# Chunks of 128, 256, 44 times 512 and 384 tokens in a fused RG-LRU and FFN kernel, with the first twenty chunks ordered anew

## The chip, the cores and the metric

The kernel runs on one core of one Trainium2 chip. The metric is the device time of one execution in microseconds (us); the smaller, the better. A core has five engines that run their own instruction streams in order and meet at semaphores: PE (TensorE, the matrix multiplier), DVE (VectorE), ACT (ScalarE), POOL (GpSimd) and SP (SyncE, which here only issues DMAs).

## The reference

Two stages. First a gated linear recurrence over the tokens of each of 4 sequences of 5,824 tokens and 256 channels, then a feed-forward network (FFN) over all 23,296 tokens without an activation function:

```python
sig_r = 1.0 / (1.0 + np.exp(-r_gate))
sig_i = 1.0 / (1.0 + np.exp(-i_gate))
log_a = c * sig_r * np.log(np.clip(a_base, 1e-06, 1.0 - 1e-06))[None, None, :]
a_t = np.exp(log_a)
norm = np.sqrt(np.maximum(1.0 - a_t * a_t, 1e-06))
x_gated = norm * sig_i * x
for t in range(S):
    h = a_t[:, t] * h + x_gated[:, t]
    y[:, t] = h
...
a = x @ w1
b = x @ w2
h = a * b @ w3
return (h @ w_out).astype(np.float32)
```

In the second part `x` is the `y` of the first. w1 and w2 are 256 x 1024, w3 is 1024 x 1024, w_out is 1024 x 256. Since nothing stands between w3 and w_out, the kernel multiplies them once ("the fold", wp = w3 @ w_out) and uses the product. Inputs and output are float32, the matrix products run in bfloat16.

## The kernel before

The tokens are cut into chunks (`sizes`, L50). For each chunk a chain of jobs runs, and each job has a letter:

- `r`, `i`, `x` (L133) load the three inputs with one DMA each. `R` and `I` take the tanh on ACT (the sigmoid is made of it), `p` adds 1 on POOL, `t` multiplies by x in two halves on POOL (for the chunks in `DV_TIMES` in one step on DVE; halves in `DV_HALF` on DVE).
- `V` and `U` turn the results from tokens on partitions to channels on partitions. The chunks in `TURN_R` and `TURN_U` are turned on PE, by transposes of 128 x 128 into PSUM (L180); the others by one DMA transpose (L192).
- `d` (exp, ACT) makes the decay a, for each of two blocks of 128 channels; `s` squares it (POOL, or DVE or ACT by the sets `DV_SQUARE` and `AC_SQUARE`); `q` takes the root (ACT, with another function table, so a table load stands before it and another after it); `g` multiplies (DVE); `h` is the scan on DVE, which starts from the last column of the chunk before; `y` casts to bfloat16 on POOL (`DV_CAST`, `AC_CAST`: on DVE or ACT).
- `a` and `b` multiply by w1 and w2 on PE. The 1,024 hidden columns are four pairs of 128-column blocks; `ac.m.q` fills one PSUM slot with one block, `bc.m` fills two. `c` copies a's block out of PSUM (ACT, or DVE for `DV_COPY`), and `m` multiplies it by b's on DVE. `D` multiplies 128 tokens by wp, 8 matmuls of 256 columns; `e` copies two such results out (ACT, or DVE for `DV_EVAC`), `o` stores them.
- `L`, `C` load and cast the weights; `Ft`, `Fc`, `Fm`, `Fe` do the fold for one of 8 row blocks of w3: transpose, copy, multiply, scale into wp. `W` is a run of 8 matmuls without use, put where PE would wait.

Two things rule what runs when. `ORDER` (L438) is one written list of all jobs: each engine executes its own jobs in exactly this order, so a job that waits holds up all that follows on its engine. And `RINGS` (L102) says how many buffers a kind of tile has: the turned r and u, the a blocks, the D results and the fold's results share four PSUM slots ("po"), the b results and W share two ("pb"), the loads have four or five. A job that takes a buffer waits until the job that last read it is done. The weights pass through the buffers of a and nrm.

SP issues every DMA, in order. Its queue holds the loads, the DMA transposes and the stores.

The first chunks hold 256 tokens each, the last 256. wp must be complete before the first `D`, so the early part of the kernel is the FFN's first half for chunks 0 to 2, the fold and the gates of the next chunks.

Of the kernel before, what the change touches and what calls it, by code (L numbers as in the profile page):

```python
# [22 lines left out]
def kernel(  # L23
# [26 lines left out]
    sizes = [256, 256] + [CT] * 44 + [256]  # L50
# [29 lines left out]
    TURN_R = {0, 1, 2, 3, 4, 7, 12}  # L80
    TURN_U = {0, 1, 2, 3, 4, 5, 6, 7}
    DV_TIMES = {0, 1}
    DV_PLUS = set()
    DV_HALF = {(2, 0)}
    DV_SQUARE = {(0, 0), (1, 0), (10, 0)}
    AC_SQUARE = {(1, 1), (2, 0), (2, 1), (3, 0), (4, 0), (4, 1), (6, 0), (8, 1), (9, 1), (11, 0), (11, 1), (12, 1),
        (13, 0), (13, 1), (14, 0), (14, 1), (15, 1)}
    DV_CAST = set()
    AC_CAST = {4}
    DV_COPY = {(0, 0, 0), (0, 1, 0), (0, 1, 1), (0, 3, 0), (1, 1, 0), (1, 1, 1), (1, 2, 0), (1, 2, 1), (1, 3, 0), (2,  # L90
        0, 1), (2, 1, 0), (2, 1, 1), (2, 3, 0), (3, 0, 1), (3, 2, 0), (3, 2, 1), (4, 0, 0), (4, 1, 0), (4, 2, 0), (4, 2,
        1), (5, 1, 1), (5, 2, 1), (6, 2, 0), (6, 2, 1), (6, 3, 1), (7, 0, 0), (7, 1, 1), (7, 3, 0), (7, 3, 1), (8, 1, 0),
        (8, 2, 0), (9, 1, 0), (9, 1, 1), (9, 2, 1), (10, 0, 0), (10, 1, 0), (10, 1, 1)}
    DV_EVAC = {(1, 0), (2, 0), (3, 1), (5, 1), (9, 0), (9, 1)}
    FOLD_ACT = {('c', 7), ('e', 0), ('e', 1), ('e', 2), ('e', 3), ('e', 7)}
    W_ACT = {('w2', 0), ('w3', 6)}
    W_DVE = {('w1', 1)}
    STAGE = {'w1': ['a', 'a'], 'w2': ['nrm', 'nrm'], 'wo': ['a', 'nrm'], 'w3': ['a', 'nrm', 'a', 'nrm', 'a', 'nrm',
        'a', 'nrm']}
    CASTING = set()  # L100
    WARM = [8, 8, 8, 8, 8, 8, 8, 8, 8, 8, 8, 8, 8, 8, 8, 8]
# [59 lines left out]
    def times(c, half):  # L161
        n = sizes[c] // P
        fused = c in DV_TIMES
        if half == 0 or fused:
            T["u", c] = ring(gates, [P, NCB, 4, P], BF16, name="u_t", tag="u")
# [34 lines left out]
    def decay(c, cb):  # L200
        w = sizes[c]
        if cb == 0:
            T["a", c] = ring(held, [P, NCB, CT], F32, name="a_t", tag="a")
        a, pr = T["a", c][:, cb, :w], T["pr", c][:, cb, :w]
        if long_rows(c):
            a, pr = in_time(a), turned(pr)
        nc.scalar.activation(out=a, in_=pr, func=AF.Exp, scale=la4[:, cb:cb + 1], bias=la4[:, cb:cb + 1])  # L207

    def square(c, cb):
        w = sizes[c]  # L210
        if cb == 0:
            T["n", c] = ring(held, [P, NCB, CT], F32, name="nrm", tag="nrm")
# [23 lines left out]
    def scan(c, cb):  # L236
        w = sizes[c]
        if cb == 0:
            T["h", c] = ring(ypool, [P, NCB, CT], F32, name="h_t", tag="h")
        h, a, n = (T[key, c][:, :, :w] for key in "han")  # L240
        if cb == 0:
            for b in range(1, B):
                if 0 < b * S - starts[c] < w:
                    nc.vector.memset(a[:, :, b * S - starts[c]:b * S - starts[c] + 1], 0.0)
# [47 lines left out]
    def product(c, mp):  # L292
        w = sizes[c]
        if mp == 0:
            T["g", c] = ring(ffn, [P, KD, CT], BF16, name="g_t", tag="g")
        nc.vector.tensor_mul(out=T["g", c][:, 2 * mp:2 * mp + 2, :w], in0=T["sa", c, mp][:, :, :w],  # L296
                             in1=T["pb", c, mp][:, :, :w])

    def down(c, j):
        if c == NCH - 1:  # L300
            T["po_last", j] = po = ring(psum_o, [P, D], F32, name="po", tag="po")
        else:
            if j % 2 == 0:
# [7 lines left out]
    def evac(c, j2):  # L311
        T["ot", c, j2] = ring(ffn, [P, 2, D], F32, name="ot", tag="ot")
        copy_to((c, j2) in DV_EVAC, T["ot", c, j2], T["po", c, j2])

    def evac_last(c, j):
        if j % 2 == 0:
# [7 lines left out]
    def store(c, j2):  # L324
        t0 = starts[c] + 2 * j2 * P
        nc.sync.dma_start(out=out[t0:t0 + 2 * P, :].rearrange("(j p) c -> p j c", p=P),
                          in_=T["ot", c, j2])
# [36 lines left out]
    def fold_t(mi):  # L364
        pt = ring(psum_o, [P, KD, P], BF16, name="ptw", tag="po")
# [51 lines left out]
    def last(c):  # L417
# [21 lines left out]
        r0 r1 E A3. A0. A1. i1 R1 R0 W3 V1 I1 V0 W13 W12 A2. W9 d1.0 d1.1 s1.0 i0 W15 I0 x0 t0.1 W14 d0.0 s0.0 s1.1  # L439
        d0.1 s0.1 q0 x1 t1.1 Lw1.0 r3 Lw2.0 r2 q1 R3 Lw1.1 i2 W11 U0 g0 h0.0 Lw2.1 Cw1.0 W10 W2 U1 W0 W7 R2 W4 h0.1  # L440
        Lw3.2 x2 g1 y0 W8 Lwo.0 Cw2.0 a0.1.0 a0.1.1 h1.0 c0.1.0 h1.1 a0.0.0 a0.0.1 V2 c0.1.1 d2.0 c0.0.0 W6 y1 b0.0
        c0.0.1 d2.1 I2 Cw1.1 a1.0.1 a1.0.0 b0.1 a1.1.0 a0.2.0 c1.0.0 c1.0.1 Cw2.1 p2 a0.2.1 Cw3.2 m0.0 m0.1 c1.1.0
        Lwo.1 b1.0 m1.0 t2.0 r4 W1 c0.2.0 a1.1.1 a0.3.0 t2.1 Cwo.0 W5 c1.1.1 Ft2 c0.2.1 a1.3.0 s2.0 b1.1 c0.3.0 b0.2
        U2 a1.3.1 s2.1 Cwo.1 i3 Fc2 V3 x3 Lw3.0 q2 Lw3.1 i4 Lw3.4 m1.1 c1.3.0 Fm2 R4 g2 h2.0 h2.1 d3.0 Lw3.7 c1.3.1
        m0.2 d3.1 Lw3.5 Fe2 a1.2.0 a0.3.1 b1.2 a1.2.1 I3 c0.3.1 V4 s3.0 d4.0 d4.1 b0.3 y2 c1.2.0 Cw3.0 c1.2.1 m1.2
        a2.0.0 a2.1.0 b1.3 m0.3 a2.2.0 b2.0 m1.3 a2.2.1 c2.0.0 Lw3.3 a2.0.1 s4.0 c2.2.0 s3.1 p3 t3.0 c2.1.0 Cw3.1 Ft0
        c2.0.1 c2.2.1 Fc0 m2.0 Cw3.4 b2.1 I4 s4.1 q4 r7 t3.1 a2.3.0 a2.1.1 Fm0 b2.2 p4 Cw3.5 c2.1.1 Ft4 c2.3.0 m2.1
        Fe0 Ft1 a2.3.1 U3 Lw3.6 q3 Fc4 c2.3.1 Fc1 Fm4 Cw3.7 b2.3 Ft5 g3 Fe4 Fc5 Ft7 x4 Cw3.3 R7 r5 h3.0 h3.1 Fm1 Fm5
        Fc7 Fe5 Ft3 Fm7 Fe1 Cw3.6 V7 Fe7 y3 Ft6 Fc3 d7.0 d7.1 Fc6 m2.2 Fm3 i6 r6 a3.1.0 Fe3 R5 Fm6 a3.1.1 c3.1.0
        c3.1.1 t4.0 Fe6 t4.1 i7 i5 x5 U4 a3.0.0 R6 D0.0 a3.0.1 D0.1 I6 c3.0.0 e0.0 m2.3 g4 a3.3.0 a3.2.0 b3.0 h4.0  # L450
# [24 lines left out]
        D9.0 b11.3 D9.1 a12.0.1 m11.2 D9.2 m11.3 D9.3 b12.0 y13 x17 R18 d17.0 c12.0.0 c12.0.1 e9.0 m12.0 I17 a12.2.0
# [133 lines left out]
```

## Time and profile before

| | us |
|---|---|
| median of 3 runs | 516.77 |
| lowest and highest run | 515.22, 517.76 |
| span of the profiled execution | 513.8 |
| PE, ACT, DVE, POOL busy in it | 499.8, 465.5, 430.6, 312.9 |
| first FFN matmul starts | 12.97 |
| last store lands | 513.8 |

The profile shows one execution, instruction by instruction. Its span runs from the first to the last instruction; for this execution no other time is given, and the median of the runs is 3.0 us above the span. A row of the timeline is: start, length, engine, line, operation, output and inputs, shapes, how many were merged, and in brackets the idle time of the engine before it with what ended it. `L268` is line 268. Busy time is the time in which an instruction of the engine is under way, though two may overlap. In the first 60 us, the DMA view shows 280 to 425 GB/s from 3 us to about 44 us.

### The profile page before, as it was taken

Reading aid. Unit: us, or ns where it says so; the run is one execution under the profiler, and the core shown is the slowest. Engines: PE = TensorE matmul, PEld = TensorE weight load, DVE = VectorE, ACT = ScalarE, POOL = GpSimd, SP = SyncE. Lnnn points to the kernel's source line nnn. Section 1 sums busy time; section 2 is a strip of 40 time slices with the busy share of each in tenths; the row PEclk is TensorE's granted clock in tenths of the full one; section 3 lists DMA queues with packets and bytes.
Section 4 is the critical chain, followed back from the end, with each engine's and each line's share of the span. In section 5 each row is a group of like instructions: output and inputs, shape, how many; then the busy total and the mean of one; then the engine's idle time right before and its main releaser. Section 6 shows DMA issues by size and latency. Waiting matters only on the chain.

```text
span 513.8 us, 9036 instructions
## 1 busy us (share of the span) xinstructions
PE 499.8 (97%) x3267; PEld 314.2 (61%) x3321; DVE 430.6 (84%) x414; ACT 465.5 (91%) x720; POOL 312.9 (61%) x271
## 2 busy tenths in 40 slices
PE   7889999999999999999999999999999999999997
PEld 7658565566565566556656556564566655656566
DVE  5889999999999889978878799888878697959762
ACT  8899999999999999999999999998998979888543
POOL 2583858646637956866595983957646569480200
PEclk9999999999999999999999999999999999999999
DMA  8997999999989998896999996989795995252112
GB/s 299 410 414 255 305 315 285 312 240 316 314 242 269 266 276 261 221 276 201 289 288 310 262 272 191 234 228 246 197 265 132 215 316 170 101 150 76 54 60 103
DMA packets 177281, 123.82 MB, mean 241 GB/s; under 512 B 86354, under 2 KB 172884, under 8 KB 177236
## 3 DMA queue, kind: packets, MB, share of 16 engines
q1 hardware_dynamic: 177232, 123.23, 84.6%
q8 instruction: 26, 0.43, 0.3%
q14 instruction: 19, 0.16, 0.1%
q10 hardware_dynamic: 4, 0.00, 0.0%
HBM read 78.91 MB, written 23.86 MB: 200 GB/s over the span
## 4 chain that ended last, share of the span: by engine, by line
PE 86%; ACT 5%; DMA 4%; issue 2%; DVE 2%; SPq 1%; ACTq 0%; DVEq 0%
PE po L307 29%; PE pb L268 28%; PE pa L268 27%; DMA r_t<-in_r_gate_dram 4%; ACT sa L284 2%; PE pw L378 1%; PE ptr L185 1%; DVE g_t L296 1%; PE ptw L367 1%; ACT ot L284 1%; SPq L136 1%; DVE h_t L249 1%; ACT i_t L154 1%; ACT a_t L207 1%; ACT L154 0%
## 5 line engine op out<-in xcount | busy, mean ns | idle before, releaser
L296 DVE TENSOR_TENSOR g_t<-sa,pb 128x1024 bf16<-128x1024 bf16 (+1 forms) x188 | 219.0, 1181 | 62.0 <-PE pb L268 29.1
L268 PEld LDWEIGHTS <-w_sb 128*128 128x128 bf16 x1504 | 146.3, 98 | 146.8 <-issue 5.5
L284 ACT CAST sa<-pa 128x512 bf16<-128x512 f32 (+1 forms) x339 | 182.4, 588 | 27.6 <-PE pa L268 18.3
L268 PE MATMUL pa<-y_t,w_sb 128*128 128x512 bf16 (+1 forms) x721 | 185.9, 372 | 4.5 <-ACT sa L284 3.5
L268 PE MATMUL pb<-y_t,w_sb 128*128 128x512 bf16 (+1 forms) x729 | 182.5, 372 | 1.5
L307 PE MATMUL po<-wp_sb,g_t 128*128 128x256 bf16 x1456 | 177.7, 273 | 0.4
L307 PEld LDWEIGHTS <-g_t 128*128 128x128 bf16 x1456 | 142.4, 98 | 40.5 <-issue 0.9
L258 POOL CAST y_t<-h_t 128x1024 bf16<-128x1024 f32 (+1 forms) x46 | 51.2, 1112 | 141.2 <-DVE h_t L249 138.8
L178 POOL TENSOR_TENSOR u_t<-i_t,x_t 128x512 bf16<-128x512 f32 (+1 forms) x89 | 120.0, 1365 | 5.5 <-DMA ut<-u_t 2.5
L249 DVE TENSOR_TENSOR_SCAN h_t<-a_t,h_t,nrm 128x512 f32<-128x512 f32 (+1 forms) x92 | 121.0, 1345 | 1.9
L217 POOL TENSOR_TENSOR nrm<-a_t 128x512 f32<-128x512 f32 (+1 forms) x74 | 81.3, 1116 | 12.8 <-ACT a_t L207 9.9
L207 ACT ACTIVATE a_t<-rt,la 128x512 f32<-128x512 bf16 (+1 forms) x80 | 64.2, 821 | 0.0
L159 POOL TENSOR_SCALAR i_t<-i_t 128x1024 f32<-128x1024 f32 (+1 forms) x45 | 53.4, 1189 | 17.6 <-ACT i_t L154 17.6
L284 ACT COPY ot<-po 128x512 f32<-128x512 f32 (+1 forms) x85 | 49.6, 590 | 11.8 <-PE po L307 11.5
L232 DVE SCALAR_TENSOR_TENSOR nrm<-nrm,ut 128x1024 f32<-128x1024 f32 (+1 forms) x39 | 54.4, 1394 | 5.2 <-ACT nrm L221 5.2
L154 ACT ACTIVATE i_t<-i_t 128x1024 f32<-128x1024 f32 (+1 forms) x47 | 49.2, 1049 | 0.1
L221 ACT ACTIVATE nrm<-nrm 128x1024 f32<-128x1024 f32 (+1 forms) x47 | 48.4, 1040 | 0.2
L147 ACT ACTIVATE th_r<-r_t 128x1024 bf16<-128x1024 f32 (+1 forms) x40 | 42.6, 1065 | 0.0
L282 DVE CAST sa<-pa 128x512 bf16<-128x512 f32 (+1 forms) x37 | 21.9, 617 | 1.4 <-PE pa L268 1.1
L221 ACT ACT_TABLE_LOAD x17 | 21.8, 1283 | 0.4
L215 ACT ACTIVATE nrm<-a_t 128x512 f32<-128x512 f32 (+1 forms) x17 | 10.7, 648 | 0.1
L263 PE MATMUL warm<-ident 128*128 128x128 bf16 x128 | 10.2, 247 | 0.0
(57 smaller groups left out, 132.6 us busy)
## 6 DMA issues: line engine op xcount, KB each, us to landing
out_dram<-ot SPq DMA_DIRECT2D x90, 256.0 KB, 3.4
r_t<-in_r_gate_dram SPq DMA_DIRECT2D x44, 512.0 KB, 5.3
i_t<-in_i_gate_dram SPq DMA_DIRECT2D x44, 512.0 KB, 5.9
x_t<-in_x_dram SPq DMA_DIRECT2D x44, 512.0 KB, 5.9
wf<-in_moe_w_dram SPq DMA_DIRECT2D x12, 512.0 KB, 10.1
wf<-in_moe_w_out_dram SPq DMA_DIRECT2D x2, 512.0 KB, 10.5
r_t<-in_r_gate_dram SPq DMA_DIRECT2D x3, 256.0 KB, 2.7
i_t<-in_i_gate_dram SPq DMA_DIRECT2D x3, 256.0 KB, 3.8
```

Of the source, the lines that this page charges most:

```text
L154: nc.scalar.activation(out=t[:, :n, :], in_=t[:, :n, :], func=AF.Tanh, scale=0.5)
L159: (nc.vector if c in DV_PLUS else nc.gpsimd).tensor_scalar(t, t, 1.0, 1.0, op0=ALU.add, op1=ALU.mult)
L178: (nc.vector if (c, half) in DV_HALF else nc.gpsimd).tensor_mul(out=u, in0=t, in1=xt)
L207: nc.scalar.activation(out=a, in_=pr, func=AF.Exp, scale=la4[:, cb:cb + 1], bias=la4[:, cb:cb + 1])
L217: (nc.vector if (c, cb) in DV_SQUARE else nc.gpsimd).tensor_mul(out=n, in0=a, in1=a)
L221: nc.scalar.activation(out=T["n", c][:, :, :w], in_=T["n", c][:, :, :w], func=AF.Sqrt, scale=-1.0, bias=1.0)
L232: nc.vector.scalar_tensor_tensor(out=T["n", c][:, :, :w], in0=T["n", c][:, :, :w], scalar=1e-3, in1=T["pu", c][:, :, :w], op0=ALU.max, op1 ...
L249: nc.vector.tensor_tensor_scan(h[:, cb, :], a[:, cb, :], n[:, cb, :], init, ALU.mult, ALU.add)
L268: nc.tensor.matmul(out=dst[:, :w], lhsT=w_sb[:, cb, m * P:(m + 1) * P], rhs=T["y", c][:, cb, :w], start=(cb == 0), stop=(cb == NCB - 1))
L284: nc.scalar.copy(out=dst, in_=src_ps)
L296: nc.vector.tensor_mul(out=T["g", c][:, 2 * mp:2 * mp + 2, :w], in0=T["sa", c, mp][:, :, :w], in1=T["pb", c, mp][:, :, :w])
L307: nc.tensor.matmul(out=po, lhsT=T["g", c][:, k, j * P:(j + 1) * P], rhs=wp_sb[:, k, :], start=(k == 0), stop=(k == KD - 1), skip_group_che ...
```

## The change

The chunk sizes become 128, 256, 44 times 512 and 384, and the list of jobs and the sets that name engines are other ones for chunks 0 to about 20. From there to chunk 45 the list is as before, shifted by 128 tokens. The code that handles sizes is widened: a tile is made by whichever job comes first, and the results of an odd number of 128-token blocks may be copied and stored one at a time.

```diff
-    sizes = [256, 256] + [CT] * 44 + [256]
+    sizes = [128] + [256] + [512] * 44 + [384]
...
-    TURN_R = {0, 1, 2, 3, 4, 7, 12}
-    TURN_U = {0, 1, 2, 3, 4, 5, 6, 7}
+    TURN_R = {0, 1, 2, 3, 4, 5, 6, 7}
+    TURN_U = {0, 1, 2, 3, 4, 7}
...
-    DV_HALF = {(2, 0)}
-    DV_SQUARE = {(0, 0), (1, 0), (10, 0)}
+    DV_HALF = {(4, 0)}
+    DV_SQUARE = {(0, 1), (1, 0), (6, 0), (12, 0)}
...
-    DV_CAST = set()
-    AC_CAST = {4}
+    DV_CAST = {2}
+    AC_CAST = {0, 13}
...
-    FOLD_ACT = {('c', 7), ('e', 0), ('e', 1), ('e', 2), ('e', 3), ('e', 7)}
-    W_ACT = {('w2', 0), ('w3', 6)}
-    W_DVE = {('w1', 1)}
+    FOLD_ACT = {('c', 7), ('e', 0), ('e', 3), ('e', 4), ('e', 6)}
+    FOLD_DMA = set()
+    W_ACT = {('w1', 0), ('wo', 0)}
+    W_DVE = {('w1', 1), ('w2', 0), ('w3', 3)}
...
+    def pair(c, j2):
+        return min(2, sizes[c] // P - 2 * j2)
...
     def evac(c, j2):
+        k = pair(c, j2)
         T["ot", c, j2] = ring(ffn, [P, 2, D], F32, name="ot", tag="ot")
-        copy_to((c, j2) in DV_EVAC, T["ot", c, j2], T["po", c, j2])
+        copy_to((c, j2) in DV_EVAC, T["ot", c, j2][:, :k], T["po", c, j2][:, :k])
```

`AC_SQUARE` has 17 entries before and after, other ones; `DV_COPY` grows from 37 to 44, `DV_EVAC` has six in both. `WARM` is unchanged in value, and `FOLD_DMA`, with its branch in `fold_t`, is empty. The beginning of `ORDER`, up to the first matmul of chunk 2:

```diff
-        r0 r1 E A3. A0. A1. i1 R1 R0 W3 V1 I1 V0 W13 W12 A2. W9 d1.0 d1.1 s1.0 i0 W15 I0 x0 t0.1 W14 d0.0 s0.0 s1.1
-        d0.1 s0.1 q0 x1 t1.1 Lw1.0 r3 Lw2.0 r2 q1 R3 Lw1.1 i2 W11 U0 g0 h0.0 Lw2.1 Cw1.0 W10 W2 U1 W0 W7 R2 W4 h0.1
-        Lw3.2 x2 g1 y0 W8 Lwo.0 Cw2.0 a0.1.0 a0.1.1 h1.0 c0.1.0 h1.1 a0.0.0 a0.0.1 V2 c0.1.1 d2.0 c0.0.0 W6 y1 b0.0
...
+        r0 i0 i1 r1 x0 Lw1.0 x1 Lw2.0 i2 r2 x2 Lw1.1 Lw2.1 A3. E A0. A1. A2. R0 I1 I0 R1 W0 W7 W14 V0 V1 d0.1 s0.1
+        d0.0 d1.0 d1.1 s1.0 t0.1 t1.1 s0.0 q0 W9 W12 U0 W13 W3 U1 W1 W2 W10 g0 h0.1 h0.0 s1.1 q1 g1 h1.1 Cw1.0 y0
+        a0.0.1 W8 W11 a0.0.0 a0.1.1 W4 h1.0 y1 a1.0.0 W15 c0.0.1 Cw2.0 b0.0 a1.0.1 c0.1.1 c0.0.0 m0.0 a1.1.1 c1.0.0
+        c1.0.1 I2 R2 V2 d2.1 s2.1 d2.0 s2.0 q2 a0.1.0 c0.1.0 c1.1.1 a1.1.0 c1.1.0 b1.1 b0.1 m1.1 m0.1 b1.0 W5 Cw1.1
+        m1.0 a1.3.1 a1.3.0 a1.2.0 p2 t2.0 t2.1 Cw2.1 Lw3.2 Cw3.2 Lwo.0 Lwo.1 Cwo.1 r3 r4 a0.3.1 b1.3 c1.3.1 c1.3.0
+        m1.3 U2 W6 b0.3 a0.3.0 c1.2.0 Cwo.0 c0.3.0 c0.3.1 Ft2 g2 Fc2 m0.3 R3 a0.2.0 a0.2.1 a1.2.1 Fm2 b0.2 c0.2.1
+        c0.2.0 R4 b1.2 V3 c1.2.1 V4 h2.0 h2.1 y2 Lw3.4 Lw3.1 Lw3.0 i3 Lw3.5 x3 r7 Lw3.7 Lw3.3 d3.0 d3.1 s3.1 d4.0 d4.1
+        s4.1 I3 Cw3.4 s4.0 s3.0 Cw3.1 Cw3.0 q3 p3 Fe2 a2.0.1 a2.0.0 m0.2 b2.0 m1.2 c2.0.0 c2.0.1 a2.1.0 b2.1 c2.1.0
...
```

## The prediction

> **What bounds the kernel now.** I read the busy shares first, then the chain of waits, then the timeline of the first 50 us, and last the sums by window.
>
> ```profile
> span 513.8 us, 9036 instructions
> PE 499.8 (97%) x3267; PEld 314.2 (61%) x3321; DVE 430.6 (84%) x414; ACT 465.5 (91%) x720; POOL 312.9 (61%) x271
> ...
> PE 86%; ACT 5%; DMA 4%; issue 2%; DVE 2%; SPq 1%; ACTq 0%; DVEq 0%
> ```
>
> PE (TensorE) holds 86% of the chain, so I ask how much of PE's time the result doesn't need. The chain in order of time (start, length, what) gives the early part that isn't PE and, further on, the spacing of back-to-back matmuls:
>
> ```profile
> 5.24 8.59 DMA r_t<-in_r_gate_dram
> 13.91 10.40 DMA r_t<-in_r_gate_dram
> 24.37 1.28 ACT L145
> 25.67 1.06 ACT th_r L145
> ...
> 37.07 0.89 PE ptw L367 x16
> ...
> 63.22 1.73 PE pb L268 x8
> ...
> 122.34 3.49 PE po L307 x32
> ```
>
> A 128-column matmul takes 0.0555 us, a 256-column one 0.109, a 512-column one 0.216. Work that must be done: 1456 512-column equivalents of "up" (314.5 us), 1456 "down" matmuls (158.9), the weight fold with 64 transposes and 64 matmuls (10.5), 104 turning transposes (5.8): 489.7 us. The last matmul ends at 510.7, so PE loses about 21 us before that, and 3.1 us of stores follow. Where the 21 us go is in the timeline:
>
> ```profile
> 12.97 1.03 PE L268 MATMUL pa<-y_t,w_sb 128*128 128x256 bf16 x8
> ...
> 18.99 0.38 PE L268 MATMUL pa<-y_t,w_sb 128*128 128x256 bf16 x2 [1.10 <-ACT sa L284]
> ...
> 24.37 1.28 ACT L145 ACT_TABLE_LOAD   x1 [1.18 <-DMA r_t<-in_r_gate_dram]
> 25.67 1.06 ACT L145 ACTIVATE th_r<-r_t 128x1024 bf16<-128x1024 f32 x1
> ...
> 27.70 0.38 PE L268 MATMUL pa<-y_t,w_sb 128*128 128x256 bf16 x2 [2.19 <-ACT sa L284]
> ...
> 30.21 1.47 ACT L207 ACTIVATE a_t<-ptr,la 128x512 f32<-128x512 bf16 x2
> 31.53 0.62 ACT L284 CAST sa<-pa 128x512 bf16<-128x512 f32 x1
> ```
>
> Up to 27.70 the timeline has 56 needed matmuls of 256 columns (6.1 us) and 48 transposes (2.7): 8.8 us of needed work, so 18.9 us are lost there; the remaining 2 us or so are spread over 480 us in pieces under 0.4. The last early stall is a DMA's: r4 lands at 24.3, the tanh of chunk 4 stands ahead of the copies on ACT, and PE waits 2.19 us. After 27.7 PE never stops. So the change can gain only before 27.7 us, and lose anywhere.
>
> ```profile
> 100.00:150.00 50.00, 49.74 (x305) 30.32 (x310) 47.94 (x48) 49.48 (x73) 29.40 (x28) 1.00 1.03 291
> ```
>
> From 50 to 350 us ACT (fourth pair) is busy 95 to 99% and DVE (third) 96% here, beside a PE without gaps. That looks like no slack at all.
>
> **Two rules of the skill, weighed.** "ScalarE: Activation LUTs", section "What ACT_TABLE_LOAD costs", says that back-to-back activations overlap by about 93 ns. The trace agrees: two exps at 30.21 last 1.47 us, but the next instruction starts 1.32 later, 0.66 apiece for a mean of 0.82 in the groups. So I step ACT at duration minus 0.1 (DVE minus 0.06: three scans and products start 1.1 to 1.2 apart for 1.2 to 1.26), and ACT's 73 instructions in the window above hold about 42 of 50 us. The slack is real. The same section prices a table switch at 2.66 us including a drain; here the load at 24.37 is followed by its tanh 1.30 later, and I go by 1.30. "Perfetto Trace Analysis", section "Identifying the Most-Contended Engine", calls matmul busy time a poor measure; PE's 97% here includes the modelled ends of warm-up matmuls, which is why I count matmuls instead.
>
> **The change, part by part.**
>
> *Turning.* TURN_R gains chunks 5 and 6 and loses 12; TURN_U loses 5 and 6. Transposes on PE: 104 to 92, 12 x 0.0555 = -0.67 us, on the path since PE has no gaps. In their place come three DMA transposes and two go, on SP's queue. U5 stands behind the stores o2.0 and o0.0; estimated from the DVE and ACT rows it is issued by 53 us (behind it wait o1.0, r10, i8 and V8, none wanted before 60), a transpose lands some 5 us later (the DMA view of the first 60 us has a median of 4.9), and chunk 5's first matmul follows 24 us of PE work after 42. Covered; without cover each would cost up to 5 us.
>
> *Loads.* The instants at which consumers stop waiting for a DMA give arrival against bytes queued before (units of 128 KB): r1, 4 units, 3.87; x0, 10, 7.23; w1's first half, 16, 10.08; r2, 28, 13.85; w2's second, 40, 17.97; r4, 60, 24.31: about 0.32 us a unit. In the new order r0 is 1 unit, r1 6, x0 7, the first w1 11, r2 25, x2 29, w1's second 33, r3 53, r4 57. Interpolated: r1 5.0, w1 8, r2 12.9 (before 13.85), x2 14.2 (before, 48 units, about 20.5), r4 23.2. Two loads wait for staging buffers on SP: wo's first half for w1's cast on ACT (10.2, no later than its turn), w3's piece 4 for the second w1 cast on DVE (about 17.5); behind it stand six weight pieces, i3 and x3, but four loads issued earlier run until 23.2, so the engines don't empty: 0.
>
> *Start.* ACT: tanh of 128 tokens at 3.2 us, the gates of chunks 0 and 1 until 7.2, table load to 8.5, roots to 9.3, w1's cast (0.94) to 10.2, y0's cast 0.3. First FFN matmul about 10.7 instead of 12.97. But chunk 0 holds only 128 tokens, and until chunk 2 only 384 tokens can be multiplied instead of 512; this step alone buys nothing.
>
> *Path to chunk 2.* From r2 at 12.9: tanh 0.95; V2 with its two hops 0.85; two exps and two squares on ACT 2.7; table 1.30; root 0.95; a copy, wo's cast and two copies 1.6; table 1.30; R3 0.95; two copies 0.4; R4 0.95; V4 0.6. Sum 12.55: 25.5. The other branch, x2 14.2, u on POOL (2 x 1.3), w2's cast (1.0), b1.3, U2, gating 1.2, the fold's copy and a product 0.9, two scans 2.4, y2 on DVE 0.7, with their hops, gives 24.8 to 25.6. DMA no longer ends a wait here; ACT does. By then the needed work is 384 tokens up (5.3), 44 transposes (2.4), one fold block (1.3): 9.0. Lost: 16.5, against 18.9. Bounds: a POOL product at 1.71 (20.97 of the trace shows one) and 0.1 more per hop make it 17.8; arrivals 0.3 earlier make it 16.2. I take 16.5, a gain of 2.4.
>
> *25 to 46 us.* Seven fold blocks, chunk 2's matmuls and three turns, 17 us of PE work, share four PSUM slots of the ring "po", each released by ACT or DVE. Stepped at the spacing above, PE waits nowhere over 0.3 us: tight are U3 (POOL's second product of chunk 3), V7 (the copy c2.3.1 after I5), V5 (behind d7.1). With full durations instead of spacings, those waits sum to 2.3 us. Before loses 0.3 there. I take +0.5, range 0 to +2.3.
>
> *Engine loads.* DVE: 6 copies of 512 more (3.7), two weight casts (1.4), y2 (0.7), a fold scaling (0.4), a square (0.65) and small ones: about +7 us. ACT: 13 copies of 256 and 6 of 512 fewer, 8 of 384 and 4 of 128 more, about -3 us. On the path at 0 if DVE's spare spacing covers it; products (L296) hold pb, so uncovered it is PE's loss.
>
> *Tail.* The last chunk has three down groups instead of two, covered by PE's order as before; the stores of 128 tokens after the last copy are the same. 0, bounds +-0.3. The `not in T` tests, pair(), the empty FOLD_DMA and WARM change no instruction's price.
>
> Sum: -0.7 - 2.4 + 0.5 = -2.6 at the span, rounded to -2.5 for the hops left out. Span 511.3. The profile has no other time for its execution than the span; the median of the three runs lies 3.0 above it, a part that the change doesn't touch, so 514.3.
>
> **Rivals.**
>
> *Gain given back* (same): the order on ACT (tanhs and exps of chunks 5 to 9 ahead of copies) lets PE wait between 25 and 70 us at full-duration prices, +2 instead of +0.5. For: ACT works without a pause from 12 us. Against: the measured overlap. 516.77 - 0.7 - 2.4 + 2.3 = 516.0; with smaller gains up to 518.
>
> *DVE becomes the bound* (slower): in the 105 us after 45 us, DVE idles about 3.5 us by busy time, and about 4.5 us of its new work falls there (four copies, a square, a half of u). If busy time rather than spacing is what it can't exceed, products come late, pb (two buffers) isn't freed, and PE stops at the b's: 1 us of overflow plus waits at each of ten chunks' g and scan, estimated 3 to 6 with the early gain gone in part. It decides once DVE's added work exceeds 3.5 us. 516.77 + 3 = about 520.
>
> *It doesn't act:* the order moves the start, but r4 at 23.2 only saves 1.1 us against 24.3, so that 1.1 + 0.7 is all: 515.0. This lies inside the first case's range.
>
> **How the numbers follow.** Gain kept, 515.5 or less: 0.58. Given back, to 518.5: 0.24. DVE, above: 0.18. Range 512.3 to 518.9. A measurement here can tell 0.5%, 2.58 us, from no change. The forecast lies almost on that bound, so case one splits into 0.43 and 0.15; with 0.23 of the second, same is 0.38, and slower is the third case and a rest of 0.01. Below 512.3 I leave 0.07, above 518.9 0.12.
>
> **What would show it.** Right: first pa near 10.7, first chunk-2 matmul (512 wide) near 25.5, 92 ptr matmuls, no PE idle over 0.4 after 26, PE's last matmul near 508. Wrong: PE rows at L268 or L307 waiting on ACT sa between 27 and 60 by more than 2 us in all (rival one), or on DVE g_t after 50 (rival two), or r2's tanh after 14.

## The result, and the profile after

| | before | after |
|---|---|---|
| median of the runs, us | 516.58 (4 runs) | 520.13 (4 runs, 519.56 to 520.41) |
| ratio to before, 95% interval | | 1.0068 [1.0046, 1.0090] |
| span of the profiled execution, us | 513.8 | 518.3 |
| first FFN matmul / first 512-wide one, us | 12.97 / 29.54 | 12.54 / 28.67 |
| last matmul ends, us | 510.7 | 515.2 |

The change makes the kernel slower by 3.55 us, where 2.5 us of gain were forecast. The medians mix two granted clocks of PE: of 100 further runs of before, made beside the experiments, 42 had a mean clock of 1.000 and a median of 515.62 us, 58 one of 0.996 to 0.997 and a median of 517.14 us. After's four runs all had 1.000, and so had both profiled executions. At equal clock the change costs 4.5 us (520.13 against 515.62), as the two spans say.

The page's head, busy row and chain of the kernel after:

```profile
span 518.3 us, 9021 instructions
PE 501.7 (97%) x3256; PEld 312.9 (60%) x3309; DVE 433.3 (84%) x426; ACT 464.1 (90%) x713; POOL 315.4 (61%) x266
...
PE 75%; DVE 12%; ACT 4%; issue 4%; DMA 2%; POOL 1%; SPq 0%; DVEq 0%; POOLq 0%; ACTq 0%
```

The busy row says next to nothing: PE is again at 97%. The chain does: PE's share falls from 86 to 75% and DVE's rises from 2 to 12%, so the chain now runs through other engines more often. Where, the sums by window tell (stretch, its length, then busy time of PE, PEld, DVE, ACT and POOL, clock, DMA share, GB/s), first of after, then of before:

```profile
28.00:46.00 18.00, 17.01 (x164) 12.33 (x164) 17.87 (x26) 17.26 (x24) 11.83 (x11) 1.00 1.05 401
46.00:76.00 30.00, 29.79 (x212) 19.65 (x214) 28.88 (x33) 29.94 (x44) 17.68 (x15) 1.00 0.87 260
76.00:156.00 80.00, 77.33 (x464) 45.48 (x470) 77.88 (x80) 76.23 (x110) 50.47 (x43) 1.00 1.03 282
```

```profile
28.00:46.00 18.00, 17.90 (x172) 13.45 (x173) 15.43 (x24) 17.05 (x26) 13.76 (x14) 1.00 1.03 398
46.00:76.00 30.00, 29.79 (x207) 19.46 (x210) 29.35 (x32) 29.81 (x42) 18.90 (x18) 1.00 1.00 275
76.00:156.00 80.00, 79.49 (x495) 48.32 (x502) 76.89 (x79) 79.39 (x118) 48.88 (x44) 1.00 1.03 280
```

Two places lose: the start up to 46 us, and 76 to 156 us, where PE is busy for 77.33 instead of 79.49 us and ACT, too, does less. The clock is 1.00 in all six rows.

For all kernels I use one sum, the **loss**: an instant minus the time that the needed matmuls up to it take at the prediction's prices. Some matmul records are missing from most traces; with them filled in from the written list, the values come out up to 0.2 us lower up to 46 us, 0.4 at 75 and 0.6 at 150. The last column needs no records: at the last matmul all the needed work is done, 489.7 us before and 489.0 after.

| loss (us) at | 28 | 46 | 75 | 150 | last matmul (ends at) |
|---|---|---|---|---|---|
| before | 18.92 | 19.24 | 19.47 | 20.36 | 21.0 (510.7) |
| after | 19.21 | 20.73 | 20.98 | 24.87 | 26.2 (515.2) |

In all, 5.2 us more are lost, and 0.67 comes off for the turns: 4.5 us, the shift of the last matmul. By 46 us the start has lost 1.5 us more than before's; the stretch from 75 to 150 us loses 3.0 more (3.89 against 0.89; 3.4 with the missing records filled in), the rest 0.7 (or 0.3).

What PE waits for from 76 to 156 us, in the view of waits of after (engine, line, waited for, total us, times, longest); the same view of before names nothing:

```profile
PE pa L271 <- POOL y_t L261: 1.0, 3, 0.6
PE pa L271 <- DVE sa L285: 0.6, 2, 0.4
PE pa L271 <- DVE ot L285: 0.3, 1, 0.3
PE pb L271 <- DVE g_t L299: 0.3, 1, 0.3
```

Seven small waits make 2.2 us; the rest of the 3.9 us is in gaps below what this view lists.

**The start of after.** Its timeline, DVE first, then PE, then ACT, shows how the early gain was lost:

```profile
10.19 0.69 DVE L177 SCALAR_TENSOR_TENSOR u_t<-i_t,x_t 128x512 bf16<-128x512 f32 x1 [1.83 <-DMA x_t<-in_x_dram]
10.80 0.48 DVE L231 SCALAR_TENSOR_TENSOR nrm<-nrm,ptr 128x128 f32<-128x128 f32 x2
11.31 0.74 DVE L252 TENSOR_TENSOR_SCAN h_t<-a_t,nrm 128x128 f32<-128x128 f32 x2
...
12.54 0.27 PE L271 MATMUL pa<-y_t,w_sb 128*128 128x128 bf16 x2
...
15.43 0.38 PE L271 MATMUL pa<-y_t,w_sb 128*128 128x256 bf16 x2 [1.05 <-POOL y_t L261]
...
14.77 1.04 ACT L147 ACTIVATE th_r<-r_t 128x1024 bf16<-128x1024 f32 x1
17.39 0.78 ACT L209 ACTIVATE a_t<-ptr,la 128x512 f32<-128x512 bf16 x1 [1.59 <-PE ptr L187]
...
28.67 1.04 PE L271 MATMUL pa<-y_t,w_sb 128*128 128x512 bf16 x3 [0.27 <-ACT a_t L209]
```

x1 is issued behind the first half of w1 and lands at 10.17 us. DVE waits 1.83 us for it, with chunk 0's gating and scans queued behind; this is one reason why the first FFN matmul comes at 12.54, not 10.7. Then r2's tanh starts at 14.77, its transposes wait behind a1.0.0 on PE, which waits for POOL's y1, and the exps start at 17.39.

### The profile page after: what moved, and what is told of

Same layout as the page of the kernel before. It is cut to its first block, busy times and chain, and to the rows that moved or that the text cites. A ratio compares the mean times of both kernels' runs of the same rounds, so it can differ in the third digit from the quotient of the medians.

```text
span 518.3 us, 9021 instructions
## 1 busy us (share of the span) xinstructions
PE 501.7 (97%) x3256; PEld 312.9 (60%) x3309; DVE 433.3 (84%) x426; ACT 464.1 (90%) x713; POOL 315.4 (61%) x266
## 4 chain that ended last, share of the span: by engine, by line
PE 75%; DVE 12%; ACT 4%; issue 4%; DMA 2%; POOL 1%; SPq 0%; DVEq 0%; POOLq 0%; ACTq 0%
PE pa L271 25%; PE po L313 25%; PE pb L271 24%; DVE h_t L252 4%; DVE g_t L299 3%; ACT sa L287 2%; DVE sa L285 2%; DVE nrm L234 1%; DMA x_t<-in_x_dram 1%; POOL y_t L261 1%; DVE nrm L231 1%; PE pw L389 1%; ACT nrm L223 1%; DVE ot L285 0%; PE ptw L378 0%
## 5 line engine op out<-in xcount | busy, mean ns | idle before, releaser
L299 DVE TENSOR_TENSOR g_t<-sa,pb 128x1024 bf16<-128x1024 bf16 (+3 forms) x188 | 218.9, 1181 | 64.1 <-PE pb L271 28.8
L287 ACT CAST sa<-pa 128x512 bf16<-128x512 f32 (+2 forms) x332 | 179.2, 589 | 30.9 <-PE pa L271 20.9
L271 PE MATMUL pa<-y_t,w_sb 128*128 128x512 bf16 (+2 forms) x726 | 187.4, 372 | 5.1 <-POOL y_t L261 2.0
L271 PE MATMUL pb<-y_t,w_sb 128*128 128x512 bf16 (+3 forms) x725 | 181.6, 372 | 2.5 <-DVE g_t L299 1.0
L261 POOL CAST y_t<-h_t 128x1024 bf16<-128x1024 f32 (+2 forms) x44 | 50.8, 1154 | 140.9 <-DVE h_t L252 136.5
L180 POOL TENSOR_TENSOR u_t<-i_t,x_t 128x512 bf16<-128x512 f32 x89 | 123.9, 1408 | 6.5 <-issue 3.5
L252 DVE TENSOR_TENSOR_SCAN h_t<-a_t,h_t,nrm 128x512 f32<-128x512 f32 (+2 forms) x90 | 117.9, 1339 | 1.6
L219 POOL TENSOR_TENSOR nrm<-a_t 128x512 f32<-128x512 f32 (+2 forms) x73 | 80.9, 1126 | 18.8 <-ACT a_t L209 18.8
L156 ACT ACTIVATE i_t<-i_t 128x1024 f32<-128x1024 f32 (+3 forms) x47 | 48.7, 1040 | 2.1 <-DMA i_t<-in_i_gate_dram 2.1
L223 ACT ACTIVATE nrm<-nrm 128x1024 f32<-128x1024 f32 (+3 forms) x47 | 48.1, 1042 | 0.2
L285 DVE CAST sa<-pa 128x512 bf16<-128x512 f32 (+2 forms) x44 | 25.5, 610 | 0.6 <-PE pa L271 0.4
L209 ACT ACTIVATE a_t<-ptr,la 128x512 f32<-128x512 bf16 (+2 forms) x16 | 10.7, 710 | 1.6 <-PE ptr L187 1.6
(58 smaller groups left out, 134.7 us busy)
```

What stands on the lines that cost most here:

```text
L180: (nc.vector if (c, half) in DV_HALF else nc.gpsimd).tensor_mul(out=u, in0=t, in1=xt)
L219: (nc.vector if (c, cb) in DV_SQUARE else nc.gpsimd).tensor_mul(out=n, in0=a, in1=a)
L223: nc.scalar.activation(out=T["n", c][:, :, :w], in_=T["n", c][:, :, :w], func=AF.Sqrt, scale=-1.0, bias=1.0)
L252: nc.vector.tensor_tensor_scan(h[:, cb, :], a[:, cb, :], n[:, cb, :], init, ALU.mult, ALU.add)
L261: eng.tensor_copy(out=T["y", c][:, :, :w], in_=T["h", c][:, :, :w])
L271: nc.tensor.matmul(out=dst[:, :w], lhsT=w_sb[:, cb, m * P:(m + 1) * P], rhs=T["y", c][:, cb, :w], start=(cb == 0), stop=(cb == NCB - 1))
```

## The experiments

All ratios are to the kernel before, measured beside it, with their 95% intervals; where the granted clock matters, runs of like clock are compared as well. One profile carries some noise of its own in the start: four kernels with the same first 46 us (e1, e7, e12, e13) have their first 512-wide matmul at 27.88, 27.58, 27.56 and 26.80 us; r2 landed at 14.03, 12.75 and 13.14 us in e1, e12 and e13.

**e1, x1 first** (in after's list):

```diff
-        r0 i0 i1 r1 x0 Lw1.0 x1 Lw2.0
+        r0 i0 i1 r1 x0 x1 Lw1.0 Lw2.0
```

> The changed kernel with one load moved: x of chunk 1 is issued before the first half of w1 instead of after it. Theory L (the lead-in: the product of chunk 1 waits on DVE for x1 until 10.2 us, and the gating and scans of chunk 0 are queued behind it): x1 lands near 8, first FFN matmul near 11.7 instead of 12.5, first 512-column matmul near 27 instead of 28.7, time 1.0 to 1.8 us below the changed kernel. Theory D (DVE's own work between 75 and 150 us sets the end): an earlier start is given back there, PE's loss after 75 us grows by what the start gains, time within 0.4 of the changed kernel.

Measured: 519.30 us, 1.0047 [1.0031, 1.0063]; span 517.1. x1 lands at 7.77 us, the first FFN matmul starts at 11.86, the first 512-wide one at 27.88; the loss at 46 us is 19.70 instead of 20.73 and the gain stays to the end (25.0 against 26.2). The first FFN matmul comes as expected; the first 512-wide one and the time gain less. By the times alone, 0.8 us, the intervals overlap, and one pair of profiles is near the noise: e2 below, whose start is after's, has lost 19.92 us at 46 us by the same sum. Its first FFN matmul starts at 12.57, though, while those of e1, e7, e12 and e13, with x1 first, start at 11.28 to 12.27. The place of x1 explains up to about 1 us of the start and nothing of the stretch from 75 to 150, which loses 3.85 here.

**e2, DVE relieved** (after; ACT or POOL takes over eight jobs of DVE) and **e3, both**:

```diff
-    DV_COPY = {..., (8, 1, 1), (9, 0, 1), (9, 1, 1), (10, 3, 1), ...}
-    DV_EVAC = {(0, 0), (4, 0), (7, 1), (8, 1), (9, 1), (11, 0)}
-    DV_SQUARE = {(0, 1), (1, 0), (6, 0), (12, 0)}
+    DV_EVAC = {(0, 0), (4, 0), (11, 0)}
+    DV_SQUARE = {(0, 1), (1, 0), (6, 0)}
```

> The changed kernel with eight jobs of chunks 7 to 12 taken off DVE: four copies and three evictions to ACT, one square to POOL, about 4.9 us of DVE work. Theory D: PE's loss between 75 and 150 us falls from about 4 us to under 1.5, time 2.5 to 3.5 below the changed kernel. Theory S (DVE instructions with two SBUF inputs are stretched while POOL works, by 1.1 us at 95 us, and this sets the loss): the stretches stay, time 0 to 1.0 below.

> Both edits together. If the lead-in and DVE's work are two separate losses, the gains add: 3.5 to 5.0 us below the changed kernel, at or just below the kernel before. If one hides the other, no more than the better of the two alone.

Measured: e2 522.30 us, 1.0106 [1.0077, 1.0135]; e3 521.18 us, 1.0085 [1.0062, 1.0109]. Both are slower than the same kernel without the relief, by 2.3 and 2.7 us of span. PE's rows of e2 say why:

```profile
106.30 1.17 PE L267 MATMUL pa<-y_t,w_sb 128*128 128x512 bf16 x4 [0.48 <-ACT sa L283]
109.87 1.02 PE L267 MATMUL pa<-y_t,w_sb 128*128 128x512 bf16 x4 [1.53 <-ACT sa L283]
111.72 0.59 PE L267 MATMUL pa<-y_t,w_sb 128*128 128x512 bf16 x2 [0.83 <-DVE sa L281]
```

The copies come later from ACT than they came from DVE: from 76 to 156 us DVE's busy time falls from 77.88 to 71.55 us and PE's from 77.33 to 75.25. Both expectations for e2 failed. A test that takes load from one engine by giving it to another can't say what the load costs on the first; e7 takes it away.

**e4, DVE loaded more** (before; eight such jobs given to DVE, some 4.9 us):

```diff
+    DV_COPY: (7, 2, 1), (8, 2, 1), (9, 2, 0), (10, 2, 1)
+    DV_EVAC: (7, 1), (8, 1), (10, 1)
+    DV_SQUARE: (12, 0)
```

> The kernel before with eight more jobs of chunks 7 to 12 on DVE: four copies and three evictions from ACT, one square from POOL, about 4.9 us. Theory D: DVE, 96% busy there, can't take them; PE, which lost 0.3 us there, loses 3 to 5 and the time is 3 to 5 above the kernel before. Theory S: DVE has room at the spacing of its instructions; time within 1.0 of the kernel before.

Measured: 524.98 us, 1.0161 [1.0134, 1.0187], 7.9 us more for 4.9 us of work; in the profiles the last matmul ends 8.7 us later than before's, and all of that arises between 95 and 150 us. The longest waits, and the sums of the stretch behind the last of them:

```profile
134.07 1.02 PE L265 MATMUL pb<-y_t,w_sb 128*128 128x512 bf16 x4 [1.70 <-DVE g_t L293]
138.32 0.59 PE L265 MATMUL pa<-y_t,w_sb 128*128 128x512 bf16 x2 [2.80 <-DVE sa L279]
...
139.10:142.50 3.40, 3.40 (x10) 1.22 (x8) 1.22 (x1) 1.75 (x3) 2.90 (x3) 0.50 0.37 132
```

Just behind the wait of 2.80 us PE's clock is 0.50 for 3.4 us, which doubles the price of its matmuls and makes about 1.7 of the 8.7 us. All four runs had a mean clock of 0.993 to 0.997. Without that, some 7 us are left for 4.9: in an order not made for it, a job moved to DVE costs more than its own duration. The "spare spacing" that the prediction hid DVE's additions in is not there for just any place.

**e5, the sizes alone** (before's order and sets) and **e6, the order alone** (before's sizes):

```diff
# e5, on the kernel before
-    sizes = [256, 256] + [CT] * 44 + [256]
+    sizes = [128] + [256] + [512] * 44 + [384]
# e6, on the kernel after
-    sizes = [128] + [256] + [512] * 44 + [384]
+    sizes = [256, 256] + [CT] * 44 + [256]
```

> The new sizes (128, 256, 44 times 512, 384) under the order and the engine sets of before; the two jobs of the missing turn are dropped and the three of the last chunk's third pair of blocks are added. If the order and the engines found anew carry the loss (DVE's 4.7 us of added jobs and their places), this runs as before, 516 to 517.5 us, with some 19.5 to 20 us of TensorE lost by 50 us and under 1 us more by 150 us; it might gain up to 1 us from the smaller first chunk. If the sizes themselves carry it (chunk 2 and all after it come 128 tokens earlier against the same loads), it loses 2 to 4 us: 519 to 521.

> The order and the engine sets of after under the sizes of before (256, 256, 44 times 512, 256); the second turn of chunk 0 is put back and the last chunk's third pair is dropped. If the order and engines carry the loss, this is as slow as after, 519.5 to 522 us, with 3 us or more of TensorE lost between 76 and 150 us. If the sizes carry it, it runs as before, 516 to 518.

| | time, us | ratio | loss at 46 | 75 | 150 | first 512-wide at | needed PE work before it |
|---|---|---|---|---|---|---|---|
| before | 516.58 | 1 | 19.24 | 19.47 | 20.36 | 29.54 | 10.52 |
| e5, sizes | 519.36 | 1.0053 [1.0040, 1.0065] | 21.58 | 22.19 | 23.44 | 29.94 | 8.59 |
| e6, order | 520.73 | 1.0086 [1.0055, 1.0116] | 20.36 | 21.18 | 24.86 | 30.39 | 10.96 |
| after, both | 520.13 | 1.0068 [1.0046, 1.0090] | 20.73 | 20.98 | 24.87 | 28.67 | 9.02 |

Each half alone costs time, and each in a place of its own. The sizes cost in the start: with the old order the first 512-wide matmul comes when it came before (29.94 against 29.54), but the two short chunks now hold 384 tokens instead of 512, so 1.9 us less work lies ahead of it, and the loss at 46 us grows by 2.3. A reservation: in e5's profile PE waits 1.99 us up to 19.14, and from 20.4 to 23.9 its clock is 0.5 (14 of its 16 runs had a mean clock of 0.993 to 0.997):

```profile
20.40:23.80 3.40, 3.37 (x26) 2.60 (x24) 2.54 (x5) 2.70 (x3) 3.40 (x4) 0.51 1.06 416
```

Before's profile has no such stretch, so part of the 2.3 may be the clock's. The times settle the total: against before's runs of like clock, beside it, the sizes cost 2.4 us both at 0.997 and below (519.40 against 517.03) and at 1.000 (two runs, 517.82 against 515.45). With the new sizes the new order brings that matmul 1.3 us forward and so pays for a good third. But it loses 3.7 us from 75 to 150 with the old sizes, as it does with the new (3.9), where before's order loses 0.9 and 1.25. The two halves don't add: 2.7 and 4.1 us by the medians, 3.55 for both. At a clock of 1.000 (0.999 included) the order alone costs 4.8 us (520.21 against 515.45, three runs), so under the new order the new sizes cost nothing more. The order's waits from 76 to 156 us under the old sizes are those of after, row for row:

```profile
PE pa L271 <- POOL y_t L261: 1.0, 3, 0.7
PE pa L271 <- DVE sa L285: 0.6, 2, 0.4
PE pb L271 <- DVE g_t L299: 0.3, 1, 0.3
PE pa L271 <- DVE ot L285: 0.2, 1, 0.2
```

**e7, DVE's jobs cut short** (e1; four copies and three evictions on DVE narrowed):

```diff
+    THIN = {(8, 1, 1), (9, 0, 1), (9, 1, 1), (10, 3, 1), (7, 1), (8, 1), (9, 1)}
...
+        n = 32 if (c, mp, q) in THIN else w
+        d = 64 if (c, j2) in THIN else D
```

> The kernel with x1 issued first, and seven of the jobs that DVE has in chunks 7 to 10 of after (four copies, three evictions) cut to 32 and 64 columns: about 4.5 us of DVE's work is left out, with nothing given to ACT (the columns left out are replaced by the pair's other half in the product, and not stored in the evictions). If DVE's load between 76 and 110 us is what TensorE waits for from 76 to 150 us, the loss there falls from 3.85 us to under 1 and the time from 519.3 to about 516. If the order on ACT (five roots in a row near 100 us) or the casts on POOL decide, at least 2.5 us of the loss stays and the time is 518 to 519.

Measured: 518.08 us, 1.0028 [1.0019, 1.0038], 1.2 us below e1 (1.0 by the ratios) for 4.5 us of DVE's work left out and given to nobody. From 75 to 150 us 2.90 are lost instead of 3.85, and by the times of DVE's products (DVE's records are complete) chunk 45 is 0.8 us ahead of e1's, of which 0.3 was there at chunk 6, ahead of all jobs cut. The waits for DVE's copies are gone, those for POOL's y_t, DVE's ot and g_t stay:

```profile
PE pa L272 <- POOL y_t L262: 0.7, 2, 0.5
PE pa L272 <- DVE ot L286: 0.3, 1, 0.3
PE pb L272 <- DVE g_t L304: 0.3, 1, 0.3
```

So the load of these jobs is about a quarter of this loss. The expectation's second case came true in size, but nothing here shows that ACT's order or POOL's casts make the rest. (The five roots in a row that the expectation speaks of stand at 134.7 us, not near 100.)

**e8, R4 behind one copy** (before), and **e9**, with y2 on DVE behind h2.1 as well:

```diff
-        m1.1 c1.3.0 Fm2 R4 g2 h2.0 h2.1 d3.0 Lw3.7 c1.3.1
+        m1.1 c1.3.0 Fm2 g2 h2.0 h2.1 d3.0 Lw3.7 c1.3.1 R4
```

> The kernel before with one job moved: R4 (tanh of chunk 4's gate) stands behind c1.3.1 on ACT instead of ahead of d3.0 and c1.3.1. In before, TensorE's last long wait of the start (2.19 us, at 25.5 to 27.7 us) is for c1.3.1, which stands behind R4, and R4 waits 1.18 us for its load and 1.28 for a table load. If what sets the lead-in is such a wait in one engine's queue, the first 512-wide matmul comes 0.9 us earlier (28.6; the cast y2 ends at 28.5 and ends the wait then) and the time is 515.5 to 516.2. If the loads set it, R4 and chunk 4's decay only come later and TensorE loses the same elsewhere before 95 us: 516.5 to 518.

> As the run before it, and the cast y2 moved from POOL (1.04 us) to DVE, right behind chunk 2's scans (0.69 us beside an idle POOL). If the waits in the queues set the lead-in, the first 512-wide matmul comes at about 28.1 us and the time is 515.2 to 516. If the loads do, 516.5 to 518; and if m0.2, which y2 now stands ahead of on DVE, is what TensorE needs next, nothing more is gained than without it.

Measured: e8 514.86 us (14 runs), 0.9967 [0.9956, 0.9978]; e9 515.61 us (22 runs), 0.9985 [0.9973, 0.9997]. ACT's and PE's rows of e8:

```profile
23.35 1.28 ACT L207 ACT_TABLE_LOAD   x1
24.64 0.78 ACT L207 ACTIVATE a_t<-ptr,la 128x512 f32<-128x512 bf16 x1
25.32 0.36 ACT L284 CAST sa<-pa 128x256 bf16<-128x256 f32 x1
25.57 1.07 ACT L145 ACTIVATE th_r<-r_t 128x1024 bf16<-128x1024 f32 x1
...
25.73 0.38 PE L268 MATMUL pa<-y_t,w_sb 128*128 128x256 bf16 x2 [0.36 <-ACT sa L284]
...
27.36 0.38 PE L268 MATMUL pa<-y_t,w_sb 128*128 128x256 bf16 x2 [0.81 <-ACT a_t L207]
```

Before, ACT waited 1.18 us for r4 with the table load, d3.0 and c1.3.1 behind it. Now the table load falls into that wait, the copy is done at 25.7, PE's 2.19 us become 0.36 and 0.81, and r4's tanh comes no later than it did. The first 512-wide matmul comes at 28.51, 1.03 earlier, the loss at 46 us is 18.37 instead of 19.24. By the medians the gain is 2.0 us, by these two profiles 0.5. Most of the difference is the clock: all 14 runs of e8 had 0.999 or 1.000, of before's 35 beside them 14 had 1.000 (median 515.73) and 21 had 0.996 to 0.997 (517.15). At equal clock e8 gains 0.9 us; the other 1.1 come from the lower clock that no run of e8 had. That it follows before's wait of 2.19 us, which e8 no longer has, is likely from e4 and e5, but no trace shows before at 0.997. One word moved in the list beats both kernels. e9 shows no gain on top: the product m0.2, now behind y2 on DVE, makes PE wait 0.75 us, and the first 512-wide matmul comes at 29.02.

**e10, spliced** (e1's list up to c4.0.1, then before's order, and before's engines for FFN chunks 4 and later):

```diff
-        ... a3.2.0 a4.2.0 c4.0.1 m3.1 m3.3 c4.0.0 q5 ...
+        ... a3.2.0 a4.2.0 c4.0.1 m3.1 a3.2.1 b3.2 c3.2.0 ...
```

> The order, sets and x1-first of the changed kernel's head up to about 62 us (job c4.0.1), and from there the order of before, with before's engines for the jobs of FFN chunks 4 and later and before's turns U5 and U6 on TensorE. The lead-in should be that of the kernel with x1 first (19.7 us lost at 60 us). If the new order and sets behind the lead-in carry the 3.85 us lost from 75 to 150 us, this loses 1 to 1.5 there, and the time is 516 to 517. If the sizes, and a chunk 2 that starts earlier against the loads, carry it, 3 us or more stay lost: 519 to 520. The junction itself may cost up to 1.5 us just behind 62 us, seen there.

Measured: 527.38 us, 1.0207 [1.0181, 1.0233]. The junction costs some 8 us between 50 and 75 us (PE waits 3.10 us up to 64.63, and the clock is 0.5 from 64.9 to 68.3), far more than the 1.5 allowed for, and what follows runs with 8 us more slack than the others. Nothing follows for the question.

**e11, chunk 2's path drawn forward** (e1):

```diff
-        Lw2.0 i2 r2 x2 ... a1.0.1 ... I2 R2 V2 ... m1.0 a1.3.1 ... m1.3 U2 ... g2
+        Lw2.0 r2 i2 x2 ... R2 V2 a1.0.1 ... I2 ... p2 t2.0 t2.1 U2 a1.3.1 ... g2 m1.3
```

> The kernel with x1 first, and chunk 2's path drawn forward: r2 is issued ahead of i2 (it should land at 12.8 instead of 14.0 us), R2 stands ahead of I2 on ACT, V2 ahead of a1.0.1, U2 ahead of a1.3.1 on TensorE and g2 ahead of m1.3 on DVE. If the path r2, R2, V2, decays, root, g2, scans, y2 sets the first 512-wide matmul, it comes at 26 to 27 us instead of 27.9, and if that also is what the start is worth, the loss at 46 us falls from 19.7 to 18.2 to 19 and the time to 518.0 to 518.7. If only cover is missing (the work of the two short chunks is done before), the first 512-wide matmul comes earlier but TensorE waits as long behind it: 519 to 520.

Measured: 521.93 us, 1.0102 [1.0080, 1.0124], slower than e1. r2 lands at 12.74, but the first 512-wide matmul comes at 30.57, because each step that was moved holds up others on PE:

```profile
18.47 0.38 PE L271 MATMUL pa<-y_t,w_sb 128*128 128x256 bf16 x2 [1.52 <-ACT a_t L209]
...
23.91 0.28 PE L271 MATMUL pa<-y_t,w_sb 128*128 128x128 bf16 x2 [1.61 <-DVE nrm L231]
```

Both waits are for a slot of "po" that V2's and U2's transposes, now earlier, keep until the exps and g2 have read them. In this order the earlier landing of r2 gained nothing, and the four slots ran short.

**e12, a product of POOL moved** (e1), and **e13**, with its transpose ahead in SP's queue:

```diff
# e12
-        t10.0 t10.1 c6.2.0 ... V14 U10 e6.0 d12.1 x13 i14 x12 o6.0 o6.1 V15 r16 y9 p13
+        t10.0 c6.2.0 ... V14 e6.0 d12.1 x13 i14 x12 o6.0 o6.1 V15 r16 y9 t10.1 U10 p13
# e13
+        t10.0 c6.2.0 ... V14 e6.0 d12.1 x13 y9 t10.1 U10 i14 x12 o6.0 o6.1 V15 r16 p13
```

> The kernel with x1 first, and one product of POOL (t10.1, half of u10, at 93.9 to 95.2 us) moved behind y9's cast, with U10's transpose behind it. In the runs so far DVE's g8 beside that product takes 2.31 us instead of 1.22, DVE then runs without pause up to the scans of h9, and TensorE waits 0.78 us at 106.7 us for y9, which follows them. If the stretch beside POOL causes that wait, g8 takes 1.22 us, y9 is cast 1.1 us earlier, the loss from 95 to 115 us falls from 1.87 to about 1.1 us and the time from 519.3 to 518.5. If it doesn't, y9 comes earlier but TensorE waits as long for DVE's copies and products at 107 to 112 us: 519 to 519.6; and a later u10 may make g10 late, seen as a wait for the transpose behind 112 us.

> As the run before it, with U10's transpose put ahead of i14, x12, o6.0, o6.1, V15 and r16 in SP's queue, so that it is issued at about 106.7 us, when the moved product is done, instead of at 112.8. If only the late u10 cost the run before its 3.9 us, this shows what the stretch beside POOL is worth: the loss from 95 to 115 us stays 0.8 to 0.9 us under that of the kernel with x1 first, no wait of 3.9 us follows, and the time is 518.3 to 518.8. If the place of these jobs is as tight on the other side (the transpose of chunk 15's gate and the loads behind it 1.7 us later), the gain is given back: 519.2 to 521.

In after, DVE's g8 runs beside POOL's products; POOL's row, then DVE's:

```profile
93.82 2.50 POOL L180 TENSOR_TENSOR u_t<-i_t,x_t 128x512 bf16<-128x512 f32 x2
...
95.08 2.33 DVE L234 SCALAR_TENSOR_TENSOR nrm<-nrm,ut 128x1024 f32<-128x1024 f32 x1
...
102.55 1.22 DVE L234 SCALAR_TENSOR_TENSOR nrm<-nrm,ut 128x1024 f32<-128x1024 f32 x1
```

g8 takes 2.33 us where the same operation, beside an idle POOL at 102.55, takes 1.22: about the time until POOL's second product ends (96.3) comes on top. The Trainium skill's page "SBUF — State Buffer", section "Who interferes with whom", says that DVE and POOL share one pair of ports as an exclusive lock, and that a DVE instruction with two SBUF inputs, as g8 is (nrm and ut), contends with a POOL instruction that reads SBUF; this row agrees. In e12 the product is out of the way and g8 takes 1.22 us:

```profile
93.90 1.22 DVE L234 SCALAR_TENSOR_TENSOR nrm<-nrm,ut 128x1024 f32<-128x1024 f32 x1
...
119.41 1.23 DVE L234 SCALAR_TENSOR_TENSOR nrm<-nrm,ut 128x1024 f32<-128x1024 f32 x1 [4.34 <-ACT th_r L149]
```

The loss from 105 to 115 us falls from 1.74 to 0.88, as expected. But U10 is now issued at 112.84, behind V15's transpose, so g10 at 119.41 stands 4.34 us (the view names ACT; what DVE is short of is the transpose of u10), and PE waits 3.9 us up to 122.6; from 123.1 to 126.5 its clock is 0.5, which costs up to 1.7 us more: 523.79 us, 1.0151 [1.0123, 1.0178]. e13 removes that wait: 518.82 us, 1.0046 [1.0027, 1.0064], no different from e1's 1.0047. The 0.86 us are saved up to 115 us in e13, too, but from 115 to 150 us it loses 2.16 us where e1 loses 0.96. The stretch is real, but removing it in this way gains nothing net.

## Why the prediction was wrong

**The base.** The prediction took the 3.0 us between before's span and the median of its runs as a part that the change doesn't touch. Every run of before and after for which a span is on record lies only 1.7 to 2.0 us above that span; the other 1.1 come from the runs of before at the lower clock. The profiled execution of before ran at 1.000, as all runs of after did, so the change did touch that part.

**Turning: right.** 92 ptr matmuls, 0.67 us less; U5 and U6 on DMA cause no wait.

**Loads: about 1 us too early, and one missed.** r2 landed at 13.95 in after (12.9 forecast; 12.75 to 14.03 in e1, e12 and e13), w1's first half at 9.50 (8), r4 at 24.38 (23.2). The working named x0 and x2 and left out x1, which the list puts behind w1's first half, and whose product stands first in DVE's queue. w3's piece 4 was issued at 20.5 instead of 17.5, since the second cast of w1 on DVE began at 19.6; it landed at 25.69.

**Start: wrong.** 10.7 us forecast, 12.54 measured. e1 shows the missed load to be 0.7 us of it; the rest is ACT, where roots and w1's cast follow one after the other (in e1 the cast starts at 10.48).

**Path to chunk 2: the step that failed first.** 25.5 forecast, 28.67 measured. The needed work before it, 9.0, was right (9.02), so 19.65 us are lost there instead of 16.5. Of the 3.2 us, r2's landing is 1.05. Its tanh starts 0.8 after the landing, because I2 stands ahead. From the tanh's end, 15.81, to the exps 1.6 us pass instead of 0.85, because V2 stands on PE behind a1.0.0 and that behind y1. From 17.39 the rest took 11.3 instead of 10.75. The other branch is as late: chunk 2's two scans on DVE take 3.19 us beside POOL, where the sum had 2.4, and y2 ends at 28.61. The sum took chunk 2's jobs one after the other and forgot the jobs ahead of them in each queue. The saving in the start that this step was to keep turned into a loss: in the table of e5, the 128 tokens less take 1.9 us of work (1.5 in after) from ahead of chunk 2, which pays only if it comes sooner by more than that, and it came 0.9 us sooner.

**25 to 46 us:** +0.5 in a range to +2.3; measured 1.5 against before's 0.3, so +1.2. Rival one's sign, PE waiting for ACT's sa, appears once (0.6 us, at a transpose), far from its 2 us.

**Engine loads: the other step that failed.** "On the path at 0 if DVE's spare spacing covers it" is off by 3.0 us from 75 to 150 us, and there was no such spare. The prediction took 0.1 us for each of ACT's 73 instructions from the busy time of 49.48 us and got 42 of 50: "the slack is real". But busy time counts an overlap once already. A row of before's groups from 100 to 150 us (count, busy us, mean ns) shows it:

```profile
L284 ACT CAST sa<-pa 128x512 bf16<-128x512 f32 x28 | 15.7, 598 | 0.4 <-PE pa L268 0.4
```

28 times 598 ns are 16.7 us, busy are 15.7. Counts times means of all the groups make 57.9 us; less 7.3 for the overlaps, ACT fills the whole 50. DVE's room is likewise no more than its idle time, 3.8 us from 46 to 156 us (29.35 and 76.89 of 110 us, before), less than the 4.5 us that rival two counts; so rival two's reckoning, from busy time, was the sounder one.

It named the size, too (about 520), but not the whole cause. e4 says that DVE has no room for jobs at places that weren't made for them; but e7 takes 4.5 us of that very load away and gets 0.5 to 1.2 back, about rival two's 1 us of overflow. e6 shows that the loss belongs to the new order with its sets, under either size. Of its parts, the copies and evictions on DVE are about 0.9 us up to 150 us (e7), and removing the stretch beside POOL gained nothing (e13). What makes the remaining 2 us stays open: it comes in pieces of 0.1 to 0.6 us behind y_t, g_t and evictions, and e10, meant to separate the order from the sizes behind the start, failed. One candidate that no run tests is ACT: it is busy for 79.39 of 80 us from 76 to 156 us before, so a job that comes late there finds no room to catch up, and in after it is busy for 76.23.

**Tail:** 0 forecast; with missing records filled in, after loses 1.5 us from 150 us to the end and before 1.3, which is within the 0.3 allowed.

Of the signs, r2's tanh after 14 us appeared (14.77), and so did the late first matmuls and a last matmul at 515.2 instead of 508.

## What to carry to other kernels

A smaller first chunk starts the work sooner and also leaves less of it to cover the wait for the next one: its worth is the shift of the second start minus the work taken from ahead of it. In a kernel whose engines run fixed queues, price a job by who stands ahead of it in each queue and which buffer slot it holds, and look for a wait on a load that other ready work stands behind: moving one tanh behind two jobs that were ready gained 2.0 us (0.9 at equal clock), where the whole new order lost. Don't take overlaps off a busy time: they are off already. Before two medians are compared, look at the granted clock of each run. An engine's idle share doesn't tell whether a job can be added to it or what taking one away is worth; both must be tried at the place.

## What the runs showed of the hardware

- POOL is stretched by DVE as DVE is by POOL: y1's cast on POOL took 1.19 us in after beside DVE's cast of w2, where before's took 0.61. In e12, two scans on DVE beside POOL took 3.90 us instead of 2.45.
- PE's granted clock is 0.5 for 3.4 us in four traces: e5 from 20.4, e10 from 64.9, e12 from 123.1, e4 from 139.1 us. Each time PE had waited 1.99 to 3.89 us for one job until 0.3 to 1.3 us before. In the other traces no wait behind 10 us is above 2.2 us and no such stretch occurs before the last matmul; before's own wait of 2.19 us had none in its trace.
- The same loads, issued at the same place, landed up to 1.3 us apart between executions (w1's first half at 8.96, 9.37 and 10.27 us in e12, e13 and e1). A single profile can't tell a difference in the start of less than about 1 us.
